# A fused attention and FFN kernel: seven block products for one FFN1, and a new order for batches 2 to 7

## The chip, the cores and the metric

One Trainium2 chip, one of its cores. The core has TensorE for matrix products (PE in the profile; its weight loads are PEld), VectorE (DVE), ScalarE (ACT), GpSimd (POOL, which here issues loads) and SyncE (SP, which here issues stores and transposing DMAs). SBUF is the working memory, PSUM the memory that TensorE writes: 8 banks of 512 float32 per partition. The metric is the device time of the kernel in microseconds; the median of several runs is given, and the profile shows one execution of its own.

## The reference

Attention with squared relu in place of softmax, then a two-layer FFN with a leaky relu. Cut to what matters:

```python
# q, k, v: 8 batches, 12 heads, 448 positions, head size 64
scores = scale * np.matmul(q, k.transpose(0, 1, 3, 2))
attn = np.maximum(scores, 0.0) ** 2 / S
x = np.matmul(attn, v)        # put together to 3584 tokens x 768
h = x @ w_in                  # 768 x 2048   (FFN1)
g = np.maximum(h, 0.0) + alpha * np.minimum(h, 0.0)
out = g @ w_out               # 2048 x 768   (FFN2), float32
```

## The kernel before

All products are in bfloat16 with sums in float32. The work of the eight batches is cut into pieces, and plans written as text say in which order the pieces are issued; each word of a plan issues one piece to the queues of its engines. Every engine takes its queue in order and waits where an operand or a buffer isn't ready.

**Attention.** Four heads of one batch are a quad of heads; there are 24. `load_qk` and `load_v` fetch them over POOL's queue. Before scores can be formed, q and k must lie transposed in a tile `T`. For the first five that is done on TensorE (`turn_pe`), from then on by `turn_dma` (L188): two copies, on ACT or DVE, rearrange q and k into a tile `perm` (L195; there is one such tile, three times the space of `w_mix` is used in its place), and a transposing DMA on SP's queue reads it (L197). `land` (L417) is a tiny POOL copy that waits for the landing; the loads of later quads are issued behind it on POOL. A quad has seven chunks of keys. A chunk's scores are four 64x64 products of 448 columns at once, over two PSUM banks (`score_mm`, L209); then comes the relu from PSUM, `rl`, on ACT (L218) or DVE (L220), and the square, `at`, on ACT (L229) or DVE (L231). When the seven squares are there, `attnv` multiplies them with v (28 products, L241) and two scalings write `xT` (L253 ACT, L255 DVE).

**FFN1.** Of a batch, 16 tiles of 128 hidden units: six products of 128x128 weights by 448 tokens each, into one bank (`f1_mm`, L275). Then ACT writes `neg` (L281) and DVE forms `gT` from it and from the bank (L282). 96 products per batch.

**FFN2.** Two batches share a `gT` of 896 columns, seven blocks of 128 tokens. Most blocks are taken in pairs (class `Pair`): the 2 x 2 blocks of a pair are multiplied with w_out by seven products of eight steps (384 columns each) and not eight, after Strassen and Winograd. The sums of blocks that this needs are made by DVE (`mix`, L331, and once for the weights in `weight_mix`, L313), and further DVE additions put the products together (`plus`, L340). A block that is in no pair goes through `f2` (L300). The stores go over SP's queue, 64 rows each, and near the end over ACT's too (the word `z`).

**PSUM.** The banks are given out as the plan is walked: `take_pair` and `take_bank` give the ones taken longest ago, `hold` keeps one for an accumulation.

**The order.** The first plans cover batches 0 and 1 and the first FFN2 blocks. Then come `FIRST_PAIR` for batch 2, `EACH` for batches 3, 4 and 6, `ONE_PAIR` for 5 and `LAST` for 7. In them `f` is an FFN1 tile, `cAAD` three chunks with relus on ACT, ACT and DVE, `s0D` a square, `v` an attention with its scalings, `p6` a product of the pair p with its addition, `pa` a sum, `n` or `nD` a quad's copies, transposing DMA, landing and next loads. `LAST` is batch 7's FFN1, 16 tiles, and behind it the two last pairs, 14 products. The last product is split into 256 and 128 columns (`p4e`).

Of the kernel before, what the change touches and what calls it, by code (L numbers as in the profile page):

```python
# [20 lines left out]
def kernel(  # L21
# [50 lines left out]
    paired, two_queues = [], []  # L72
# [17 lines left out]
    def hold_pair():  # L90
        lo = min((0, 2, 4, 6), key=lambda i: (max(taken[i], taken[i + 1]), i))
        taken[lo] = taken[lo + 1] = 10**9
        return lo

    def one():
        order = sorted(range(8), key=lambda i: (taken[i], i))
        free = [i for i in order if taken[i] < 10**9]
        if not paired:
            return order[0]
        mate = max(free, key=lambda i: taken[i]) ^ 1  # L100
        return mate if mate in order[:4] and taken[mate] < 10**9 else order[0]
# [86 lines left out]
    def turn_dma(n, eng="A"):  # L188
        if n in (5, 7, 8):
            w = w_mix[2 + n % 2].rearrange("p k c -> p (k c)")[:, :4 * NJ * D]  # L190
            p = w.rearrange("p (a j s d) -> p a j s d", a=2, j=NJ, s=2)
        else:
            p = perm_pool.tile([128, 2, NJ, 2, D], BF16, tag="perm", name="perm")
        for i, name in enumerate("qk"):
            (nc.vector.tensor_copy if eng == "D" else nc.scalar.copy)(p[:, i], raw.pop((n, name)).rearrange("p s j d -> p j s d"))  # L195
        t = T_pool.tile([128, 2, NJ, 128], BF16, tag="T", name="T")
        nc.sync.dma_start_transpose(out=t.rearrange("p a j c -> p (a j) c"),  # L197
                                    in_=p.rearrange("p a j s d -> p (a j s d)"))
        T[n] = t


    att, xT = {}, {}

    def score_mm(n, j):
        ps = take_pair()
# [28 lines left out]
    def attnv(n, eng="AD"):  # L234
        ps = take_pair()
        vv = vraw.pop(n)
        for j in range(NJ):
            a = att.pop((n, j))
            for r in range(2):
                for s in range(2):  # L240
# [3 lines left out]
                                     start=(j == 0), stop=(j == NJ - 1))  # L244
        b, g = divmod(n, NG)
        if g == 0:
            xT[b] = xT_pool.tile([128, NG, 2, S], BF16, tag="xT", name="xT")
        if eng == "A":
            nc.scalar.activation(xT[b][:, g], ps[:, :, :S], ACTF.Copy, scale=out_scale)
            return  # L250
        for r in range(2):
            if eng[r] == "A":
                nc.scalar.activation(xT[b][:, g, r], ps[:, r, :S], ACTF.Copy, scale=out_scale)  # L253
            else:
                nc.vector.tensor_scalar(xT[b][:, g, r], ps[:, r, :S], out_scale, None, ALU.mult)  # L255
# [15 lines left out]
    gT = singles.tile([128, KF, 2 * S], BF16, name="gT")  # L271

    def f1_mm(ps, b, ff, ks):
        for km in ks:
            nc.tensor.matmul(ps, w_in_sb[:, km // 2, km % 2, bass.ts(ff, 128)],  # L275
                             xT[b][:, km // 2, km % 2, :],
                             start=(km == 0), stop=(km == KM - 1))

    def f1_out(ps, b, ff):
        neg = neg_pool.tile([128, S], F32, tag="neg", name="neg")  # L280
        nc.scalar.activation(neg, ps, ACTF.Relu, scale=-1.0)  # L281
# [11 lines left out]
    def f2(sb, c, h, parts=None):  # L293

        first_col, width = COLS[h][0], COLS[h][1] - COLS[h][0]
        o = o_pool.tile([128, d_model - CUT], F32, tag="o", name="osb")
        for lo, hi in parts or ((0, width),):
            ps = take_bank()[:, :hi - lo]
            for ff in range(KF):
                nc.tensor.matmul(ps, gT[:, ff, bass.ts(c, 128)], w_out_sb[:, ff, first_col + lo:first_col + hi],  # L300
                                 start=(ff == 0), stop=(ff == KF - 1))
            nc.scalar.copy(o[:, lo:hi], ps)
            store(sb, c, first_col + lo, first_col + hi, o[:, lo:hi])


    def weight_mix(i, lo, hi):

        b11, b12 = w_out_sb[:, lo:hi, :NH], w_out_sb[:, lo:hi, NH:]
# [6 lines left out]
    class Pair:  # L315

        def __init__(self, a, b):
            self.a, self.b = a, b
            ga, gb = gT[:, :, bass.ts(a[1], 128)], gT[:, :, bass.ts(b[1], 128)]
            self.a11, self.a12, self.a21, self.a22 = ga[:, :KH], ga[:, KH:], gb[:, :KH], gb[:, KH:]  # L320
            self.s = {}

        def mix(self, *which):
            for i in which:
                t = self.s[2] if i == 4 else S_pool.tile([128, KH, 128], BF16, tag="S", name="S")
# [7 lines left out]
        def mm(self, ps, left, right, start):  # L333
            for i in range(KH):
                nc.tensor.matmul(ps, left[:, i], right[:, i], start=(start and i == 0), stop=(i == KH - 1),  # L335
                                 skip_group_check=not start)

        def plus(self, ps, u, keep=None):
            t = keep if keep is not None else o_pool.tile([128, d_model - CUT], F32, tag="o", name="osb")[:, :u.shape[-1]]
            nc.vector.tensor_tensor(t, ps, u, ALU.add)  # L340
            return t

        def kept(self, tag="u"):
            return u_pool.tile([128, NH], F32, tag=tag, name=tag)

        def p1(self):
            self.xb = hold()
            self.x = psum[:, self.xb, :NH]
            self.mm(self.x, self.a11, w_out_sb[:, :KH, :NH], True)
            self.m1 = self.kept("m")  # L350
            nc.scalar.copy(self.m1, self.x)

        def p2(self):
            self.mm(self.x, self.a12, w_out_sb[:, KH:, :NH], False)
            t = o_pool.tile([128, d_model - CUT], F32, tag="o", name="osb")[:, :NH]
            nc.scalar.copy(t, self.x)  # L356
            take(self.xb, 1)
            store(*self.a, 0, NH, t)

        def p6(self):  # L360
            y = take_bank()[:, :NH]
            self.mm(y, self.s[2], w_mix[1], True)
            self.u2 = self.plus(y, self.m1, self.kept())

        def p7(self):
            y = take_bank()[:, :NH]
            self.mm(y, self.s[3], w_mix[2], True)
            self.u3 = self.plus(y, self.u2, self.kept())

        def p5(self):  # L370
            self.zb = hold()
            self.z = psum[:, self.zb, :NH]
            self.mm(self.z, self.s[1], w_mix[0], True)
            store(*self.b, NH, d_model, self.plus(self.z, self.u3))

        def p4(self, parts=((0, NH),)):
            for lo, hi in parts:
                y = take_bank()[:, :hi - lo]
                self.mm(y, self.a22, w_mix[3][:, :, lo:hi], True)
                t = self.plus(y, self.u3[:, lo:hi])  # L380
                store(*self.b, lo, hi, t)

        def p4x(self, lo=0, hi=256):
            if lo == 0:
                self.o4 = o_pool.tile([128, d_model - CUT], F32, tag="o", name="osb")[:, :NH]
            y = take_bank()[:, :hi - lo]
            self.mm(y, self.a22, w_mix[3][:, :, lo:hi], True)
            self.plus(y, self.u3[:, lo:hi], self.o4[:, lo:hi])
            if hi == NH:
                store(*self.b, 0, NH, self.o4)  # L390

        def p4y(self):
            self.p4x(256, NH)

        def p4e(self):
            self.p4(((0, 256), (256, NH)))

        def p3(self):
            self.mm(self.z, self.s[4], w_out_sb[:, KH:, NH:], False)
            store(*self.a, NH, d_model, self.plus(self.z, self.u2))  # L400
            take(self.zb, 1)
# [6 lines left out]
    def prepare(n, eng="A"):  # L408
        if n < NQ:
            turn_dma(n, eng)  # L410
            land(n)
        if n + 2 < NQ:
            load_qk(n + 2)
        if n + 1 < NQ:
            load_v(n + 1)

    def land(n):  # L417
        nc.gpsimd.tensor_copy(landed, T[n][:1, 0, 0, :1])  # L418

    class Walk:  # L420

        def __init__(self):
            self.b, self.ff, self.held, self.parts, self.p, self.r, self.quad = 0, 0, [], 0, None, None, 11
# [9 lines left out]
        def step(self, w):  # L433
# [36 lines left out]
            elif c in "pr":  # L470
                if rest[0] in "abcd":
                    getattr(self, c).mix("abcd".index(rest[0]) + 1)
                else:
                    getattr(getattr(self, c), "p" + rest)()
# [3 lines left out]
            elif c == "g":  # L478
                f2(self.b // 2, int(rest[0]), int(rest[1]))
            elif c == "n":  # L480
                prepare(self.quad, rest or "A")
                self.quad += 1
# [21 lines left out]

    walk = Walk()
    walk("""Li0 Lv2 x02D x46A x24D x67A i6 t0q46D t0q24A t0q67A t0q02D t0k01D t0k24D t0k12A cA cD Lq3 cA Li1 t0k47D cA s1D t1q07D cAA s0D Li2 Lq4 s0D t1k07D cA s2D s1D Li3 y8 cAA s0D s0D cA cDA t2q07D s1D t2k05D cA s0D Lo0,0,8 s2D Lq5 Lv3 t2k57A Lo0,8 s0D Lv4 s0D cA cA cA Lv5 s0D s0D v cA v cA s0A cD e4 e1 s0D cD s0D cA s1A s1A e5 e4 e1 s0D e1 s0D v b t3q07A t3k07D E E E E""")
# [45 lines left out]
```

## Time and profile before

| | |
|---|---|
| median of 3 runs | 373.6 us (373.58 to 375.46) |
| profiled execution: span | 371.3 us |
| granted TensorE clock | 1.000 |
| PE busy | 363.6 us (98%) |
| DVE busy | 278.0 us (75%) |
| ACT busy | 274.7 us (74%) |
| POOL busy | 71.7 us (19%) |

An execution's own time holds some microseconds around the span. Busy PE is not PE at its peak: products are pipelined, and each counts as busy until its modelled end, so the pace is read from the starts. The chain of waits is followed back from the last instruction, at each step to what released it; its rows give start, length and what ran. In windows each engine's busy time in a stretch is given, with the number of instructions in brackets.

### The profile page before, as it was taken

Reading aid. Unit: us, or ns where it says so; the run is one execution under the profiler, and the core shown is the slowest. Engines: PE = TensorE matmul, PEld = TensorE weight load, DVE = VectorE, ACT = ScalarE, POOL = GpSimd, SP = SyncE. Lnnn points to the kernel's source line nnn. Section 1 sums busy time; section 2 is a strip of 40 time slices with the busy share of each in tenths; the row PEclk is TensorE's granted clock in tenths of the full one; section 3 lists DMA queues with packets and bytes.
Section 4 is the critical chain, followed back from the end, with each engine's and each line's share of the span. In section 5 each row is a group of like instructions: output and inputs, shape, how many; then the busy total and the mean of one; then the engine's idle time right before and its main releaser. Section 6 shows DMA issues by size and latency. Waiting matters only on the chain.

```text
span 371.3 us, 7894 instructions
## 1 busy us (share of the span) xinstructions
PE 363.6 (98%) x3105; PEld 197.5 (53%) x3105; DVE 278.0 (75%) x445; ACT 274.7 (74%) x406; POOL 71.7 (19%) x120
## 2 busy tenths in 40 slices
PE   8799999999999999999999999999999999999995
PEld 6454564444554565545555455554555455555563
DVE  3989988885968989566887768888749667856653
ACT  5998676877997678885997859967699866964400
POOL 8566150304211222022020220202200000000000
PEclk9999999999999999999999999999999999999999
DMA  9999989999999868455882659727646201220024
GB/s 143 188 203 202 199 135 191 153 160 167 180 171 150 123 96 163 92 89 90 160 144 64 99 80 168 144 56 121 111 89 134 49 2 43 65 65 0 0 64 108
DMA packets 73557, 43.29 MB, mean 117 GB/s; under 512 B 40368, under 2 KB 73008, under 8 KB 73520
## 3 DMA queue, kind: packets, MB, share of 16 engines
q0 software_dynamic: 27136, 22.58, 42.0%
q1 hardware_dynamic: 45712, 19.61, 25.9%
q10 hardware_dynamic: 672, 0.59, 0.5%
q8 instruction: 24, 0.39, 0.4%
q14 instruction: 13, 0.11, 0.1%
HBM read 45.62 MB, written 11.01 MB: 153 GB/s over the span
## 4 chain that ended last, share of the span: by engine, by line
PE 94%; DVE 2%; ACT 2%; issue 1%; ACTq 0%
PE psum L275 38%; PE psum L335 30%; PE psum L241 9%; PE psum L209 9%; PE psum L300 6%; PE psum L183 1%; PE psum L165 1%; DVE gT L282 1%; ACT rl L218 1%; ACT xT L253 1%; ACT neg L281 1%; DVE w_mix L195 1%; DVE T L186 0%; DVE at L231 0%; DVE osb L340 0%
## 5 line engine op out<-in xcount | busy, mean ns | idle before, releaser
L275 PE MATMUL psum<-xT,w_in_sb 128*128 128x448 bf16 x768 | 150.4, 353 | 0.2 <-DVE gT L282 0.2
L282 DVE SCALAR_TENSOR_TENSOR gT<-neg,beta_sb,psum 128x448 bf16<-128x448 f32 x128 | 85.3, 679 | 43.4 <-ACT neg L281 42.1
L218 ACT ACTIVATE rl<-psum 128x896 bf16<-128x896 f32 x128 | 111.2, 925 | 6.7 <-PE psum L209 4.7
L275 PEld LDWEIGHTS <-w_in_sb 128*128 128x128 bf16 x768 | 73.4, 98 | 73.0 <-issue 6.8
L281 ACT ACTIVATE neg<-psum 128x448 f32<-128x448 f32 x128 | 68.5, 547 | 41.0 <-PE psum L275 32.7
L231 DVE TENSOR_TENSOR at<-rl 128x896 bf16<-128x896 bf16 x105 | 62.2, 620 | 0.5 <-ACT rl L218 0.2
L229 ACT ACTIVATE at<-rl 128x896 bf16<-128x896 bf16 x63 | 58.6, 952 | 0.3
L335 PEld LDWEIGHTS <-S 128*128 128x128 bf16 x384 | 36.7, 98 | 28.4 <-issue 5.3
L335 PE MATMUL psum<-w_mix,S 128*128 128x384 bf16 x288 | 49.8, 326 | 0.2
L220 DVE TENSOR_SCALAR rl<-psum 128x896 bf16<-128x896 f32 x40 | 43.2, 1086 | 8.7 <-PE psum L209 8.1
L209 PE MATMUL psum<-T 64*64 64x448 bf16 x672 | 45.9, 357 | 2.0 <-DVE T L186 1.0
L418 POOL COPY landed<-T 1x1 bf16<-1x1 bf16 x18 | 3.3, 181 | 206.1 <-DMA T<-perm 182.9
L335 PEld LDWEIGHTS <-gT 128*128 128x128 bf16 x296 | 28.3, 98 | 20.2 <-issue 1.8
L241 PE MATMUL psum<-at,vraw 64*64 64x448 bf16 x672 | 36.6, 350 | 0.0
L335 PE MATMUL psum<-w_out_sb,gT 128*128 128x384 bf16 x192 | 34.0, 326 | 0.0
L340 DVE TENSOR_TENSOR osb<-psum,u 128x384 f32<-128x384 f32 (+2 forms) x37 | 20.2, 547 | 12.6 <-PE psum L335 8.2
L209 PEld LDWEIGHTS <-T 64*64 64x64 bf16 x672 | 17.4, 105 | 22.7 <-issue 14.8
L241 PEld LDWEIGHTS <-vraw 64*64 64x64 bf16 x672 | 21.2, 106 | 11.9 <-issue 2.9
L300 PE MATMUL psum<-w_out_sb,gT 128*128 128x256 bf16 (+1 forms) x128 | 22.0, 326 | 0.1
L255 DVE TENSOR_SCALAR xT<-psum 128x448 bf16<-128x448 f32 x24 | 14.9, 622 | 8.9 <-PE psum L241 8.3
L253 ACT ACTIVATE xT<-psum 128x448 bf16<-128x448 f32 x24 | 13.3, 556 | 9.1 <-PE psum L241 8.7
L356 ACT COPY osb<-psum 128x384 f32<-128x384 f32 x12 | 5.8, 480 | 17.4 <-PE psum L335 17.4
(45 smaller groups left out, 242.0 us busy)
## 6 DMA issues: line engine op xcount, KB each, us to landing
out_dram<-osb SPq DMA_DIRECT2D x91, 96.0 KB, 2.2
vraw<-in_v_dram POOLq DMA_DIRECT2D x24, 224.0 KB, 6.5
qraw<-in_q_dram POOLq DMA_DIRECT2D x23, 224.0 KB, 4.1
kraw<-in_k_dram POOLq DMA_DIRECT2D x23, 224.0 KB, 5.3
w_in_sb<-in_moe_w_in_dram POOLq DMA_DIRECT2D x16, 192.0 KB, 8.0
w_out_sb<-in_moe_w_out_dram POOLq DMA_DIRECT2D x4, 512.0 KB, 9.5
w_out_sb<-in_moe_w_out_dram POOLq DMA_DIRECT2D x4, 256.0 KB, 8.8
out_dram<-osb SPq DMA_DIRECT2D x8, 128.0 KB, 3.2
```

The lines of the kernel that those rows point to most:

```text
L209: nc.tensor.matmul(ps[64 * c:64 * c + 64, r, :S], t[64 * r:64 * r + 64, 1, j, 64 * c:64 * c + 64], t[64 * r:64 * r + 64, 0, :, 64 * c:64 * ...
L218: nc.scalar.activation(rl, ps[:, :, :S], ACTF.Relu)
L220: nc.vector.tensor_scalar(rl, ps[:, :, :S], 0.0, None, ALU.max)
L229: nc.scalar.activation(a, rl, ACTF.Square)
L231: nc.vector.tensor_tensor(a, rl, rl, ALU.mult)
L241: nc.tensor.matmul(ps[64 * s:64 * s + 64, r, :S], vv[64 * r:64 * r + 64, s, j, :], a[64 * r:64 * r + 64, s], start=(j == 0), stop=(j == NJ ...
L275: nc.tensor.matmul(ps, w_in_sb[:, km // 2, km % 2, bass.ts(ff, 128)], xT[b][:, km // 2, km % 2, :], start=(km == 0), stop=(km == KM - 1))
L281: nc.scalar.activation(neg, ps, ACTF.Relu, scale=-1.0)
L282: nc.vector.scalar_tensor_tensor(gT[:, ff, (b % 2) * S:(b % 2) * S + S], neg, beta_sb[:, ff:ff + 1], ps, ALU.mult, ALU.add)
L300: nc.tensor.matmul(ps, gT[:, ff, bass.ts(c, 128)], w_out_sb[:, ff, first_col + lo:first_col + hi], start=(ff == 0), stop=(ff == KF - 1))
L335: nc.tensor.matmul(ps, left[:, i], right[:, i], start=(start and i == 0), stop=(i == KH - 1), skip_group_check=not start)
L340: nc.vector.tensor_tensor(t, ps, u, ALU.add)
```

## The change

The plans for batches 0 and 1 and for the stage behind them issue the same pieces in the same order. Two things are new behind it.

First, batches 2 to 7 are one plan of some 960 words, read by a new class `Line`, in which each operation has a word of its own, with its PSUM bank: `f3` the six products of an FFN1 tile into bank 3, `N3` its `neg`, `G3` its `gT`; `c4` a chunk's scores into banks 4 and 5, `r4A` the relu on ACT, `s0D` a square; `v6` an attention, `x60A` and `x61D` its two scalings; `kqD` and `kkD` the copies of q and k, `t` the transposing DMA, the landing and the next loads; `+b63` product 6 of pair b into bank 3, `-b6` its addition or copy, `*ba` a sum. So a relu, a copy or an addition can be put anywhere among the products, and onto either engine.

Second, FFN1 of batch 7 is no longer 16 tiles of six products of 448 columns. Two tiles make a `Quad` (eight in all). Its weights are cut into 2 x 2 blocks (two tiles, two halves of the six steps) and the tokens into 2 x 2 blocks (two halves of the steps, two halves of the 448 tokens). A quad is then seven products of three steps and 224 columns. `w_in_mix` makes the sums of weight blocks (15 DVE operations; four for each of the eight quads, several at once), `tok_mix` the four sums of token blocks; they are kept in buffers whose earlier use is over. In a quad, `s`, `u` and `w` copy 224 columns of PSUM (capital letters: on DVE), `v` and `z` add on DVE, `n` is one relu of 896 columns on ACT, `g` and `h` are the two `gT`. The last two pairs of FFN2 follow as before, and the products of the two pairs before them stand among the quads'. The last product isn't split.

```diff
+    def w_in_mix(i, p, count, home):
+        a11, a12, a21, a22 = w_in_quarters(p, count)
...
+        x, y, op = {1: (a21, a22, ALU.add), 2: (made(1), a11, ALU.subtract),
+                    3: (a11, a21, ALU.subtract), 4: (a12, made(2), ALU.subtract)}[i]
+        nc.vector.tensor_tensor(t, x, y, op)
...
+    def tok_mix(i):
...
+        b11, b12, b21, b22 = x[:, :KI, :HS], x[:, :KI, HS:], x[:, KI:, :HS], x[:, KI:, HS:]
...
+        x, y, op = {1: (b12, b11, ALU.subtract), 2: (b22, tok_sum.get(1), ALU.subtract),
+                    3: (b22, b12, ALU.subtract), 4: (b21, tok_sum.get(2), ALU.subtract)}[i]
+        nc.vector.tensor_tensor(t, x, y, op)
...
+    class Quad:
...
+        def mm(self, ps, left, right, start):
+            for k in range(KI):
+                nc.tensor.matmul(ps, left[:, k], right[:, k], start=(start and k == 0), stop=(k == KI - 1),
+                                 skip_group_check=not start)
...
+            if c == "1":
+                self.mm(x[:, :HS], a11, b11, True)
+            elif c == "2":
+                self.mm(x[:, :HS], a12, b21, False)
+            elif c == "3":
+                self.mm(x[:, HS:S], self.w(4), b22, False)
+            elif c == "4":
+                self.mm(y[:, :HS], a22, tok_sum[4], False)
+            elif c == "5":
+                self.mm(x[:, HS:S], self.w(1), tok_sum[1], False)
+            elif c == "6":
+                self.mm(y[:, :HS], self.w(2), tok_sum[2], False)
+            elif c == "7":
+                self.mm(y[:, :HS], self.w(3), tok_sum[3], False)
+            elif c in "sS":
+                (nc.scalar.copy if c == "s" else nc.vector.tensor_copy)(y[:, :HS], x[:, :HS])
+            elif c in "uU":
+                (nc.scalar.copy if c == "u" else nc.vector.tensor_copy)(u[:, :HS], y[:, :HS])
+            elif c in "wW":
+                (nc.scalar.copy if c == "w" else nc.vector.tensor_copy)(u[:, HS:], y[:, :HS])
+            elif c == "v":
+                nc.vector.tensor_tensor(y[:, HS:S], x[:, HS:S], u[:, HS:], ALU.add)
+            elif c == "z":
+                nc.vector.tensor_tensor(x[:, HS:S], x[:, HS:S], u[:, :HS], ALU.add)
+            elif c == "n":
...
+                nc.scalar.activation(self.neg, psum[:, self.lo:self.lo + 2, :S], ACTF.Relu, scale=-1.0)
+            elif c in "gh":
...
+                nc.vector.scalar_tensor_tensor(gT[:, ff, (NB % 2) * S:(NB % 2) * S + S], self.neg[:, i],
+                                               beta_sb[:, ff:ff + 1], psum[:, self.lo + i, :S], ALU.mult, ALU.add)
...
+    class Line:
...
+        def do_k(self, w):
+            if self.perm is None:
+                self.perm = perm_pool.tile([128, 2, NJ, 2, D], BF16, tag="perm", name="perm")
+            copy = nc.vector.tensor_copy if w[1] == "D" else nc.scalar.copy
+            copy(self.perm[:, "qk".index(w[0])], raw.pop((self.quad, w[0])).rearrange("p s j d -> p j s d"))
+
+        def do_t(self, w):
+            n = self.quad
...
+            turn_rows(n, self.perm)
+            self.perm = None
+            land(n)
+            if n + 2 < NQ:
+                load_qk(n + 2)
+            if n + 1 < NQ:
+                load_v(n + 1)
+            self.quad += 1
...
+    P[4] = """s3D s4D s0A f0 c2 c4 s0A *ba r2A s1D c6 s0A r6D f1 f2 kqD N0 f3 kkD N2 G2 r4A f6 f7 N1 G0 N3 *bb G3 f0 N6 f2 +b63 G1 *bc G6 N0 N7 s2A c4 G0 t s0D G7
+c0 -b6 v6 r0D r4A N2 c4 G2 s1D c0 f3 r4A x60A *bd kqD f2 c4 r0A x61A r4A c0 N2 kkD f6 f7 r0D s3A G2 s1D f2 N6 c4 G6 s1A N7 s1D N2 c0 G7 f6 t r4A s1D
...
+r4A W222k W422k W144p r6A s1A f4 x21A N4 s1A f5 +h46 +h31 s2A s0D N5 s0D G4 f7 f4 v2 N0 G5 W242v -h4 f5 N7 -h3 x20D f6 x21D G0 f1 W442v N4 Q012 f0 G7
+N6 T1 G6 f7 f6 N1 W262v Q0S T2 Q06 G4 N0 f4 G1 N7 G0 N5 Q110 G7 G5 f7 f5 N6 Q1s Q02 *ic G6 N4 G4 N7 *jc N5 f6 G7 G5 f7 N7 N6 Q16 T3 +i14 T4 W462v G6
+W302 Q0u +i75 G7 Q1U -i1A +i24 -i2A *ia *ib W322 Q17 Q216 Q07 +i64 Q0W -i6 -i7 Q12 Q2s Q05 Q15 Q26 Q0v *ja *id +i54 Q2u Q03 Q0z +i45 Q04 Q1w Q1v Q0n
...
++k17 +l76 Q6g Q6h Q5n Q5g Q7n +k72 -k1A Q7g +l13 Q5h Q7h *ka +j44 *kb -j4 *la +k65 *lb -l1A -k6 +k50 -k7 +l61 *kd +k42 -k5 +k30 -k4 -l6 +l52 +k27 -k3
+-l7 -l5 +l46 *ld -k2D +l32 -l4 +l23 z -l3 -l2A"""
```

More of the change, by code (lines that the diff above doesn't have):

```diff
@@ L97, in one @@
         free = [i for i in order if taken[i] < 10**9]
[L98 to L101, printed above, removed]
+        return free[0]
     def take_bank():
@@ L271, with batches_of, may_write, may_read @@
     gT = singles.tile([128, KF, 2 * S], BF16, name="gT")
+    f1_done = {}
+    f2_done, f2_half = set(), set()
+    readers = {b: 0 for b in range(B)}
+    def batches_of(sb, c):
+        return {2 * sb + (128 * c) // S, 2 * sb + (128 * c + 127) // S}
+    for tile_no in range(B // 2 * NJ):
+        for b in batches_of(*divmod(tile_no, NJ)):
+            readers[b] += 1
+    def may_write(b, ff):
+        assert b < 2 or readers[b - 2] == 0, "gT is still read"
+        f1_done[(b, ff)] = True
+    def may_read(t, halves=(0, 1)):
+        for b in batches_of(*t):
+            for h in halves:
+                assert all((b, ff) in f1_done for ff in range(KF // 2 * h, KF // 2 * h + KF // 2)), "gT is not written"
+    def has_read(*tiles):
+        for t in tiles:
+            for b in batches_of(*t):
+                readers[b] -= 1
     def f1_mm(ps, b, ff, ks):
         for km in ks:
+            assert x_done[b] >= km // 2 + 1
+            f1_mm_done[b] = f1_mm_done.get(b, 0) + 1
             nc.tensor.matmul(ps, w_in_sb[:, km // 2, km % 2, bass.ts(ff, 128)],
@@ L291, in store, with f2_mm, f2_out, f2 @@
             eng.dma_start(out=rows[j][:, lo:hi], in_=t[64 * u:64 * u + 64])
[L293 to L303 removed]
+    def f2_mm(sb, c, h, i):
+        may_read((sb, c))
+        if (sb, c) in f2_half:
+            f2_done.add((sb, c))
+            has_read((sb, c))
+        f2_half.add((sb, c))
+        lo, hi = COLS[h]
+        for ff in range(KF):
+            nc.tensor.matmul(psum[:, i, :hi - lo], gT[:, ff, bass.ts(c, 128)], w_out_sb[:, ff, lo:hi],
+                             start=(ff == 0), stop=(ff == KF - 1))
+    def f2_out(sb, c, h, i):
+        lo, hi = COLS[h]
+        o = o_pool.tile([128, d_model - CUT], F32, tag="o", name="osb")
+        nc.scalar.copy(o[:, :hi - lo], psum[:, i, :hi - lo])
+        store(sb, c, lo, hi, o[:, :hi - lo])
+    def f2(sb, c, h):
+        i = one()
+        take(i, 1)
+        f2_mm(sb, c, h, i)
+        f2_out(sb, c, h, i)
+    mixed = [0] * 4
     def weight_mix(i, lo, hi):
+        assert not i or mixed[{1: 0, 2: 0, 3: 1}[i]] > mixed[i]
+        mixed[i] += 1
         b11, b12 = w_out_sb[:, lo:hi, :NH], w_out_sb[:, lo:hi, NH:]
@@ L331, in mix @@
                 nc.vector.tensor_tensor(t, x, y, op)
[L333 to L401, printed above, removed]
+        def run(self, name):
+            if name in "23":
+                i = self.held.pop({"2": "1", "3": "5"}[name])
+                take(i, 1)
+            elif name in "15":
+                i = self.held[name] = hold()
+            else:
+                i = one()
+                take(i, 1)
+            self.product(name, psum[:, i, :NH])
+            self.output(name)
```

272 lines of the change are left out of this document (223 added, 49 removed).

## The prediction

> **What bounds the kernel now.** I read the page's busy shares first, then the windows for the part that the change touches, then the chain of waits in that part. The change starts where batch 2 starts; in this execution that is 109.2 us after the span's start (the chain, further down, has the first products of its FFN1 there).
>
> ```profile
> PE 363.6 (98%) x3105; PEld 197.5 (53%) x3105; DVE 278.0 (75%) x445; ACT 274.7 (74%) x406; POOL 71.7 (19%) x120
> 109.20:371.30 262.10, 258.14 (x2036) 139.84 (x2032) 189.15 (x300) 187.71 (x278) 29.74 (x52) 1.00 0.51 93
> 109.20:152.50 43.30, 43.24 (x365) 23.33 (x361) 36.34 (x59) 33.24 (x49) 10.04 (x17) 1.00 0.85 139
> ```
>
> In a window the columns are the stretch, its length, then busy time of PE, weight loads, DVE, ACT and POOL, the granted clock, the DMA share and GB/s. PE is busy in 258.1 of the 262.1 us, and the 4 us that are missing lie at the end, behind its last product. The clock is 1.00. DVE has 72% and ACT 72%. In the first of these stretches DVE ran at 84% of the time (36.34 of 43.30) and PE lost nothing by it. So from batch 2 on TensorE sets the time: only fewer or shorter products, or shorter pauses between them, can shorten it, and only a pause that the new order puts in can lengthen it.
>
> A busy PE hides short pauses, because a product counts as busy until its modelled end. The chain shows them better (start, length, what). Here is one undisturbed run of attention work and one disturbed, and a second disturbed one:
>
> ```profile
> 109.25 9.19 PE psum L275 x48
> ...
> 143.82 0.53 ACT xT L253
> ...
> 176.83 0.31 PE psum L209 x4
> 177.14 1.32 PE psum L241 x28
> 178.47 0.38 PE psum L209 x8
> ...
> 186.25 0.69 PE psum L209 x12
> 186.94 1.52 PE psum L241 x28
> 188.47 0.53 ACT xT L253
> ...
> 189.04 0.97 PE psum L335 x5
> ...
> 283.61 0.69 PE psum L209 x12
> 284.30 1.50 PE psum L241 x28
> 285.80 0.70 PE psum L209 x12
> ...
> 322.40 0.53 ACT xT L253
> ...
> 331.09 18.27 PE psum L275 x96
> ```
>
> The 64x64 products of L209 and L241 go by fours, a four in 1.32 / 7 = 0.189 us. The run at 176.83 has ten fours and takes 178.47 + 0.38 - 176.83 = 2.02 us. The run at 186.25 (in the plan: three chunks, one attention, three chunks) has thirteen and takes 189.04 - 186.25 = 2.79, where 2.02 + 3 x 0.189 = 2.59 would do: a pause of 0.20, in which the chain goes over to ACT's writing of xT. The chain passes through that line four times from batch 2 on, the first at 143.82 and the last at 322.40. The run at 283.61, thirteen fours too, takes 285.80 + 0.70 - 283.61 = 2.89, a pause of 0.30. Together I count 4 x 0.20 + 0.30 = 1.1, with smaller ones **about 1.2 us of pauses**. That is all that a better order can win on PE here.
>
> **The change part by part.**
>
> *FFN1 of batch 7.* Its 96 products of 448 columns go; eight quads of seven products of three steps come, 168 of 224 columns. From the chain: 96x + e = 18.27 and 48x + e = 9.19 give x = 0.189 us a product and e = 0.11 us on coming from attention work. 224 columns don't occur; the nearest rows are these (the timeline and the groups by line):
>
> ```profile
> 10.44 0.62 PE L499 MATMUL psum<-idle 128*128 128x128 bf16 x8
> L499 PE MATMUL psum<-idle 128*128 128x128 bf16 x8 | 0.6, 220 | 0.0
> 353.09 4.06 PE L335 MATMUL psum<-w_mix,S 128*128 128x384 bf16 x24
> L335 PE MATMUL psum<-w_mix,S 128*128 128x384 bf16 x288 | 49.8, 326 | 0.2
> 366.09 1.48 PE L335 MATMUL psum<-w_mix,gT 128*128 128x256 bf16 x16
> L335 PEld LDWEIGHTS <-S 128*128 128x128 bf16 x384 | 36.7, 98 | 28.4 <-issue 5.3
> ```
>
> 128 columns: (0.62 - 0.220) / 7 = 0.057 us from start to start; 384: (4.06 - 0.326) / 23 = 0.162. The line between them gives 0.097 at 224, the line from 384 to 448 drawn on gives 0.095; I take 0.096. 168 x 0.096 = 16.1 against 96 x 0.189 = 18.2: **-2.1 us** (bounds -1.9 and -2.2). A weight load reads 98 ns, as long as such a product; but the row at 366.09 (eight products of 256 columns and eight of 128, each with weights of its own) needs (1.48 - 0.22) / 15 = 0.084, which is the line's value for their mean of 192, so the loads lie beside the products.
>
> [...]
>
> *The order of batches 2 to 7.* Each change between 64x64 and full products costs: behind a run e = 0.11, and in the run 0.69 - 3 x 0.189 = 0.12, together 0.23 us. Between the words that give PE full products, the old text has 28 runs of chunk and attention words, the new one 32. The counts of chunks (99), attentions (15), Strassen products of FFN2 (75) and FFN2 blocks (one, in two parts) are the same. So **+0.9 us**.
>
> *What DVE and ACT get.* Counted in the words: DVE takes 39 of 99 first relus, not 25, and 19 of 26 rearranging copies, not 8; five more output copies; squares stay. For batch 7 it gets 16 additions and 8 copies of 224 columns, 15 sums of w_in blocks (14 of 768 elements, one of 1536), 4 of tokens (672).
>
> ```profile
> L220 DVE TENSOR_SCALAR rl<-psum 128x896 bf16<-128x896 f32 x26 | 28.1, 1086 | 2.7 <-PE psum L209 2.3 <-issue 0.4
> L195 DVE COPY perm<-qraw 128x896 bf16<-128x896 bf16 x4 | 2.5, 612 | 0.0
> L340 DVE TENSOR_TENSOR osb<-psum,u 128x384 f32<-128x384 f32 x32 | 17.8, 557 | 10.9 <-PE psum L335 7.0 <-DMA out_dram<-osb 2.8
> L340 DVE TENSOR_TENSOR osb<-psum,u 128x256 f32<-128x256 f32 x1 | 0.4, 425 | 0.3 <-PE psum L335 0.3
> L331 DVE TENSOR_TENSOR S<-gT 128x1024 bf16<-128x1024 bf16 x22 | 14.5, 685 | 0.0
> ```
>
> 14 x 1.09 + 11 x 0.61 + 5 x 0.56 = 24.7. The 224-column ones, by the slope between 256 and 384, take 0.39: 24 x 0.39 = 9.4. The sums, scaled from 685 ns at 1024 elements, about 0.5 each, the long one 1.0: 19 of them 10. Added: some 44 us of durations; the busy time grows by less, since queued DVE operations overlap a little (I take 5 off): from 189 to about 228 of 261 us, 87%. ACT loses 14 relus and 11 copies. On the path this costs nothing as long as PE has products that don't wait for it: FFN1 tiles of batch 6 and the 14 products of pairs i and j (8 x 0.162 = 1.30 us each) stand between the quads' steps. If that cover is gone, each pause is like the 0.2 to 0.3 above. 87% is little over the 84% that the first stretch bore with no loss, so I take the same 1.2 us of pauses as before: **0** (bounds -1.2 and +5, the rivals below).
>
> *Rearranging copies, transposes, loads.* There is one perm tile, so a copy waits until the last transpose has landed. A copy that waits holds all that is queued behind it on DVE: relus, squares and gT, and so the banks that PE needs next.
>
> ```profile
> L197 SPq DMA_TRANSPOSE T<-perm x16: 1296/1532/3163, 62.3 to 292.5; - x16
> DMA to landing us min/median/max: 3.9/4.1/12.0
> ```
>
> From a transpose's issue to its landing 4.1 us pass (median). In the new text the words between a quad's second copy and the next quad's first hold at least 6.2 us of PE's work at the durations above, and at least 10 us lie before the quad's first chunk. SP issues a transpose in order among the stores, and POOL issues the next loads behind the landing, as before; none of them is late by these numbers. 0.
>
> *The end.* The old end is a product in two halves with two additions; the new one adds product 2 onto product 1 and copies 384 columns on ACT.
>
> ```profile
> 363.49 1.46 PE L335 MATMUL psum<-w_out_sb,gT 128*128 128x384 bf16 x8
> 365.03 0.48 ACT L356 COPY osb<-psum 128x384 f32<-128x384 f32 x1 [11.26 <-PE psum L335]
> 367.16 0.74 DVE L340 TENSOR_TENSOR osb<-psum,u 128x256 f32<-128x256 f32 x2 [0.26 <-PE psum L335]
> out_dram<-osb SPq DMA_DIRECT2D x91, 96.0 KB, 2.2
> out_dram<-osb ACTq DMA_DIRECT2D x3, 96.0 KB, 2.4
> out_dram<-osb SPq DMA_DIRECT2D x1, 32.0 KB, 1.9
> ```
>
> Old: PE ends at 366.09 + 1.48 = 367.57, DVE at 367.90, 0.33 later. Such a copy ended 365.51 - 364.95 = 0.56 after PE: +0.2. The last stores grow from 32 to 96 KB: +0.3 to +0.5. **+0.6 us.**
>
> Sum: -2.1 + 0.9 + 0 + 0.6 = -0.6. The profiled execution has a span of 371.3, the median of the runs is 373.6, so 2.3 lie around it. **371.3 - 0.6 + 2.3 = 373.0 us.**
>
> **The rivals.**
>
> *The pauses go.* The new order spaces chunks and their relus over four bank pairs and spares ACT, which the chain passed at the pauses. Against it: more work on DVE. 373.0 - 1.2 = 371.8, and 371.3 if the end costs only 0.2.
>
> *DVE becomes the pace-maker; slower.* Place: the attention runs, 15 with an attention. A bank pair waits for a relu of 1.09 on DVE in place of 0.92 on ACT, behind whatever the queue holds, and the attention needs its seven squares. For it: in the stretch from 61 to 71 us DVE is full and PE stands in the chain behind DVE and ACT.
>
> ```profile
> 61.00:71.00 10.00, 9.88 (x61) 4.78 (x59) 9.65 (x17) 6.90 (x13) 3.10 (x5) 1.00 1.02 154
> 68.08 1.27 DVE gT L282 x2
> 69.35 1.05 DVE w_mix L195 x2
> L218 ACT ACTIVATE rl<-psum 128x896 bf16<-128x896 f32 x75 | 65.5, 917 | 5.8 <-PE psum L209 3.8 <-ACT rl L218 2.0
> ```
>
> DVE has 9.65 of these 10 us (PE's 9.88 is by modelled ends), and from 68.08 to 70.40 the chain lies on DVE alone. Price: each of the 15 at the larger pause, 15 x 0.30 = 4.5, in place of 1.2: +3.3, 376.3. It turns the change into a loss as soon as all pauses come to more than 1.8 us.
>
> *The quads run dry; slower too.* A quad's products hang on four copies or additions between them, some 0.45 each with their hop (0.56 at 384 columns). Eight quads have 32 of them, 14 us; if a quarter finds no other product to run, +3.6: 376.6.
>
> *Weight loads set the pace of the narrow products.* One after the other at the row's 98 ns, 168 loads take 16.5 us in place of 16.1: 373.4; if each waited for the end of the product before it, 16.5 us more: 389. The 57 ns at 128 columns speak against both. [...]
>
> *The copies wait for a landing after all*: a transpose of 12.0 us, the row's maximum, against the 6.2 in hand, would hold DVE nearly 6 us once; PE's cover of perhaps half gives 376.
>
> **How the numbers follow.** Forecast (372.2 to 374.3) 0.44; the pauses go 0.29; DVE paces 0.18; quads dry 0.06; paced by loads 0.01; late landing 0.02. The range leaves out the last two and some of the outer ends: 371.3 to 376.4. 0.5% (1.9 us) is about what a measurement of this kernel can tell from no change. Faster by over that (below 371.7) is under two thirds of the second case, 0.19; slower by over that (above 375.5) most of the third to sixth and little else, 0.23; the rest 0.58.
>
> **What would show it.** Right: starts of the 224-column products 0.096 us apart; 32 runs with 0.23 of extra each; PE's last product about 1.2 us earlier and the last store landing about 0.6 us later behind it; the chain still on PE all through batches 2 to 7. Wrong: DVE lines in the chain between 109 and 330 us, PE waiting on rl or at; PE waiting on ACT or DVE copies among the quads; POOL or DVE waiting on T<-perm with PE behind them. A fall below 371 us would mean that the old order lost more between products than the chain shows.

## The result and the profile after

The new kernel takes 371.65 us (median of 7 runs, 371.28 to 372.47); the old one, in runs of the same session, 373.54. The ratio is 0.995, with a 95% interval of 0.9933 to 0.9968: faster by 1.9 us. The forecast was 373.0, in a range of 371.3 to 376.4. The result lies where the rival "the pauses go" had put it, at 371.8.

The page of the new kernel, its busy times with their shares of the span:

```profile
PE 361.2 (98%) x3169; PEld 201.7 (55%) x3169; DVE 310.9 (84%) x513; ACT 256.3 (69%) x388; POOL 73.0 (20%) x120
```

and the view of windows, the stretch from batch 2 on (same columns as before):

```profile
109.20:369.50 260.30, 255.89 (x2096) 144.04 (x2095) 222.26 (x368) 169.22 (x260) 30.53 (x52) 1.00 0.52 94
```

The span is 369.5 us, 1.8 less. From batch 2 on DVE has 222.3 of 260.3 us, 85% (72% before), ACT 65%. PE is as dense as before. So the same reading holds: what counts is the number and length of the products and the pauses between them. The chain shows both; first two attention runs, then batch 7's last quads:

```profile
188.60 0.50 PE psum L206 x8
189.10 1.32 PE psum L237 x28
190.42 0.38 PE psum L206 x8
190.80 1.24 PE psum L303 x6
...
286.33 0.69 PE psum L206 x12
287.03 1.32 PE psum L237 x28
288.35 0.38 PE psum L206 x8
288.73 1.24 PE psum L303 x6
...
342.71 3.16 PE psum L501 x33
345.87 11.71 PE psum L379 x72
```

L206, L237, L303, L379 and L501 are the new lines of chunks, attentions, FFN1 tiles, FFN2 products and quads. The run at 188.60 has eleven fours and takes 190.80 - 188.60 = 2.20 us, which is 11 x 0.189 + 0.12: no pause. The run at 286.33, the longest of the new order (three chunks, an attention, two), has twelve and takes 2.40 = 12 x 0.189 + 0.13: none either. By the starts of PE's products all 32 runs are like that. Two pauses are left, both at the opening of the stretch: 0.29 us ahead of batch 2's first FFN1 tile, which waits for `xT` (the old kernel did not pause there), and 0.23 us near 112 us. The first stands in PE's timeline, with its idle time in brackets:

```profile
109.42 1.29 PE L303 MATMUL psum<-xT,w_in_sb 128*128 128x448 bf16 x6 [0.25 <-ACT xT L249]
```

Read by the starts too, 21 of the old kernel's 28 runs are undisturbed (0.13 us over their fours), and seven pause, by 0.13 to 0.31 us, 1.57 us in all. By the chain the prediction had counted 1.2. A quad's products start 3.16 / 33 = 0.096 us apart.

So the four terms measure as follows, from the two profiled executions:

| term | forecast | measured |
|---|---|---|
| batch 7's FFN1 | -2.1 | 168 x 0.096 - 96 x 0.189 = -2.0 |
| 32 runs in place of 28 | +0.9 | 4 x 0.23 = +0.9 |
| pauses | 0 | 0.52 in place of 1.57, by the starts: -1.05 |
| the end | +0.6 | +0.4 |
| sum | -0.6 | -1.75 (spans: -1.8, medians: -1.9) |

The end, from the timeline of the new kernel:

```profile
363.91 1.46 PE L379 MATMUL psum<-w_out_sb,gT 128*128 128x384 bf16 x8
365.45 0.48 ACT L392 COPY osb<-psum 128x384 f32<-128x384 f32 x1 [13.86 <-DMA out_dram<-osb]
```

PE ends at 365.37 and the copy at 365.93, 0.56 later, as forecast (0.33 before). The bracket names the landing of an earlier store, at 365.43, as what came last before the copy; in the run of the same kernel at the end of this study it was PE, with the copy as close behind it, so the landing cost nothing here. The span ends 369.5 - 365.93 = 3.6 us behind the copy; in the old kernel it ended 371.3 - 367.90 = 3.4 behind the last addition. The larger stores cost 0.1 to 0.2, not 0.3 to 0.5.

### The profile page after: what moved, and what is told of

Same layout as the page of the kernel before. It is cut to its first block, busy times and chain, and to the rows that moved or that the text cites. A ratio compares the mean times of both kernels' runs of the same rounds, so it can differ in the third digit from the quotient of the medians.

```text
span 369.5 us, 8035 instructions
## 1 busy us (share of the span) xinstructions
PE 361.2 (98%) x3169; PEld 201.7 (55%) x3169; DVE 310.9 (84%) x513; ACT 256.3 (69%) x388; POOL 73.0 (20%) x120
## 4 chain that ended last, share of the span: by engine, by line
PE 89%; DVE 3%; ACT 3%; DMA 2%; issue 2%; SPq 1%; ACTq 0%; POOLq 0%
PE psum L303 32%; PE psum L379 28%; PE psum L206 9%; PE psum L237 9%; PE psum L330 6%; PE psum L501 4%; ACT rl L215 1%; DMA kraw<-in_k_dram 1%; DMA out_dram<-osb 1%; DVE gT L311 1%; ACT neg L310 1%; DVE w_mix L188 1%; PE psum L175 1%; SPq L320 1%; DVE T L178 0%
## 5 line engine op out<-in xcount | busy, mean ns | idle before, releaser
L303 PE MATMUL psum<-xT,w_in_sb 128*128 128x448 bf16 x672 | 134.5, 353 | 0.5 <-ACT xT L249 0.3
L215 ACT ACTIVATE rl<-psum 128x896 bf16<-128x896 f32 x114 | 100.9, 929 | 20.0 <-PE psum L206 15.9
L303 PEld LDWEIGHTS <-w_in_sb 128*128 128x128 bf16 x672 | 63.4, 98 | 65.2 <-issue 10.0
L217 DVE TENSOR_SCALAR rl<-psum 128x896 bf16<-128x896 f32 x54 | 58.5, 1086 | 11.3 <-PE psum L206 10.5
L653 ACT ACTIVATE neg<-psum 128x448 f32<-128x448 f32 x80 | 43.1, 547 | 23.7 <-PE psum L303 12.5
L659 DVE SCALAR_TENSOR_TENSOR gT<-neg,beta_sb,psum 128x448 bf16<-128x448 f32 x80 | 53.0, 676 | 7.6 <-ACT neg L653 6.4
L379 PEld LDWEIGHTS <-S 128*128 128x128 bf16 x384 | 36.7, 98 | 26.4 <-issue 3.4
L379 PE MATMUL psum<-w_mix,S 128*128 128x384 bf16 x288 | 51.0, 326 | 0.0
L206 PE MATMUL psum<-T 64*64 64x448 bf16 x672 | 46.5, 357 | 1.7 <-ACT rl L215 0.9
L435 POOL COPY landed<-T 1x1 bf16<-1x1 bf16 x18 | 4.8, 267 | 182.4 <-DMA T<-perm 158.8
L379 PEld LDWEIGHTS <-gT 128*128 128x128 bf16 x288 | 27.6, 98 | 20.0 <-issue 2.5
L237 PE MATMUL psum<-at,vraw 64*64 64x448 bf16 x672 | 36.2, 350 | 0.0
L379 PE MATMUL psum<-w_out_sb,gT 128*128 128x384 bf16 x192 | 34.9, 326 | 0.0
L396 DVE TENSOR_TENSOR osb<-psum,u 128x384 f32<-128x384 f32 x36 | 19.7, 553 | 12.0 <-PE psum L379 7.1
L206 PEld LDWEIGHTS <-T 64*64 64x64 bf16 x672 | 16.8, 105 | 23.1 <-issue 15.8
L237 PEld LDWEIGHTS <-vraw 64*64 64x64 bf16 x672 | 20.1, 107 | 12.5 <-issue 1.7
L311 DVE SCALAR_TENSOR_TENSOR gT<-neg,beta_sb,psum 128x448 bf16<-128x448 f32 x32 | 21.0, 677 | 3.9 <-ACT neg L310 3.3
L310 ACT ACTIVATE neg<-psum 128x448 f32<-128x448 f32 x32 | 17.2, 548 | 8.8 <-PE psum L303 6.1
L330 PE MATMUL psum<-w_out_sb,gT 128*128 128x512 bf16 (+1 forms) x128 | 22.0, 326 | 0.1
L249 ACT ACTIVATE xT<-psum 128x448 bf16<-128x448 f32 x28 | 15.5, 557 | 4.5 <-PE psum L237 4.5
```

What stands on the lines that cost most here:

```text
L206: nc.tensor.matmul(ps[64 * c:64 * c + 64, r, :S], t[64 * r:64 * r + 64, 1, j, 64 * c:64 * c + 64], t[64 * r:64 * r + 64, 0, :, 64 * c:64 * ...
L215: nc.scalar.activation(rl, ps[:, :, :S], ACTF.Relu)
L217: nc.vector.tensor_scalar(rl, ps[:, :, :S], 0.0, None, ALU.max)
L237: nc.tensor.matmul(ps[64 * s:64 * s + 64, r, :S], vv[64 * r:64 * r + 64, s, j, :], a[64 * r:64 * r + 64, s], start=(j == 0), stop=(j == NJ ...
L311: nc.vector.scalar_tensor_tensor(gT[:, ff, (b % 2) * S:(b % 2) * S + S], neg, beta_sb[:, ff:ff + 1], ps, ALU.mult, ALU.add)
L330: nc.tensor.matmul(psum[:, i, :hi - lo], gT[:, ff, bass.ts(c, 128)], w_out_sb[:, ff, lo:hi], start=(ff == 0), stop=(ff == KF - 1))
```

## The experiments

Two questions were open. What is each part worth by itself? And why did the pauses go, though DVE took 33 us more: because of where the operations stand, because ACT was relieved, or because 85% is still far from DVE's edge? Ratios below are to the old kernel, run beside each; the new kernel once more, at the end, gave 0.9953 (0.9934 to 0.9972).

### The order without the seven products

```diff
-            if c == "1":
-                self.mm(x[:, :HS], a11, b11, True)
+            if c in "16":
+                for km in range(KM):
+                    nc.tensor.matmul((x if c == "1" else y)[:, :S],
+                                     w_in_sb[:, km // 2, km % 2, bass.ts(2 * p + (c == "6"), 128)],
+                                     xT[NB][:, km // 2, km % 2, :], start=(km == 0), stop=(km == KM - 1))
```

and in the plan all words `W` and `T` go, and of the `Q` words all but 1, 6, n, g and h.

> The new order with batch 7's FFN1 as 16 tiles of six 448-column products, put where the quads' products 1 and 6 stood; the sums of w_in and of tokens and the quads' copies and additions are left out, all else as in the new kernel. Theory (PE sets the time, the seven products are worth their columns): PE's last product 96 x 0.189 - 168 x 0.096 = 2.05 us later, 371.65 + 2.05 = 373.7, still without pauses in the attention runs. Rival (the quads' chains and DVE work cost something that the trace hides): less than that is lost, about 1 us, 372.7.

Measured: 373.68 us, ratio 1.0002 (0.9977 to 1.0028), as the theory had it. The seven products are worth 2.0 us, what their columns say; the quads' copies, additions and sums cost nothing. And the new order without them takes as long as the old one: it buys 1.0 us of pauses with four more runs (0.9) and a longer end (0.4).

### The price of a run

The old kernel, with two runs of three chunks cut in each of batches 3, 4 and 6 (the cuts in `EACH`):

```diff
-f f f f s2A f s1D cAAA s1D f f
+f f f f s2A cA f s1D cAA s1D f f
-p6 s0D pd p7 n cA rc s1A cAA
+p6 s0D pd cA p7 n rc s1A cAA
```

> The old kernel, in whose plan for batches 3, 4 and 6 two runs of three chunks are cut into one and two chunks with a product or a tile between them: six runs more, the same operations. Theory (each change between 64x64 and full products costs 0.23 us by itself): PE's last product 6 x 0.23 = 1.4 us later, 374.9. Rival (the extra on either side is only the profile's way of marking the starts): no change, 373.5 within 0.5.

Measured: 375.67 us, ratio 1.0071 (1.0049 to 1.0092), 2.6 us slower, more than the 1.4 of six runs and far from the rival's no change. The profile shows where the rest is:

```profile
162.34 0.70 ACT rl L218
163.04 0.55 ACT neg L281
163.61 0.69 DVE gT L282
164.30 0.04 issue
164.34 3.56 PE psum L275 x18
```

Behind the cut run PE waits for a bank: a relu, a `neg` and a `gT` are done one after another before it may go on. There are three such pauses, one in each of the three batches, by the starts 0.29 us each: 1.4 + 0.9 = 2.3. So the price of a run holds, and a shifted chunk also shifts the operations behind it on ACT and DVE.

### Shorter runs in the old order

```diff
-pd cA p7 rb n p5 s2D
+pd p7 cA rb n p5 s2D
-v cAD s1D s1A s3A cA s3A r6 s2A r7
+v cAD s1D s1A s3A r6 cA s3A s2A r7
```

> The old kernel, in whose plans for batches 2, 3, 4 and 6 the last chunk of a run of three chunks, an attention and three chunks is moved behind the next product, so that no bank pair is wanted twice within a run there: four runs more. Theory (a run with six chunks pauses because banks and squares are not ready, 0.15 to 0.3 us; a shorter one does not): the four pauses go, 1.0 us, and four changes of product kind come, 0.9 us: 373.5 within 0.4, with no pause above 0.1 us in those runs. Rival (the pauses come from ACT's load, wherever the chunks stand): the pauses stay and the runs come on top, 374.5.

Measured: 373.87 us, ratio 1.0017 (1.0005 to 1.003), 0.6 us slower. The run that paused at 186.25 in the old kernel now reads so in the chain:

```profile
186.64 0.69 PE psum L209 x12
187.33 1.48 PE psum L241 x28
188.81 0.38 PE psum L209 x8
189.18 1.41 PE psum L335 x8
190.59 0.31 PE psum L209 x4
```

Twelve fours in 189.18 - 186.64 = 2.54 us: 0.15 over 12 x 0.189 + 0.12. By the starts it was 0.28 in the old kernel (the chain had shown 0.20 of it), and the four pauses together fall from 0.96 to 0.52 us. They are halved, not gone, and the single chunk at 190.59 costs its change of product kind. Neither side is right: the length of a run matters, and it isn't all.

### The new order, the old division between ACT and DVE

Fourteen `r` words and eleven `k` words get an A for their D, for example:

```diff
-c0 -b6 v6 r0D r4A
+c0 -b6 v6 r0A r4A
```

> The new order word for word, but 14 first relus and 11 rearranging copies go from DVE back to ACT, as the old plans had them (25 relus and 8 copies on DVE). Theory A (the pauses went because of where chunks, relus and scalings stand): 371.65 within 0.5, no pauses in the attention runs. Theory B (they went because ACT was relieved): pauses of 0.2 to 0.3 us come back at half of the 15 attention runs or more, at least +1.5, 373.2 or more.

Measured: 383.31 us, ratio 1.0274 (1.0258 to 1.029): 11.7 us over the new kernel. The window of that stretch:

```profile
109.20:381.10 271.90, 259.33 (x2095) 145.31 (x2095) 202.97 (x343) 187.75 (x285) 30.36 (x52) 1.00 0.49 89
```

a piece of its chain of waits:

```profile
186.13 0.34 PE psum L206 x4
...
187.31 0.93 ACT perm L693
188.24 0.83 ACT rl L215
189.07 0.04 issue
189.11 0.38 PE psum L206 x4
```

and PE in its timeline at the same place (start, duration, what, products, and in brackets the idle time before with what ended it):

```profile
187.79 0.36 PE L206 MATMUL psum<-T 64*64 64x448 bf16 x4
189.11 0.38 PE L206 MATMUL psum<-T 64*64 64x448 bf16 x4 [0.96 <-ACT rl L215]
189.43 2.77 PE L379 MATMUL psum<-w_mix,S 128*128 128x384 bf16 x16
```

A rearranging copy now stands on ACT ahead of a relu whose bank PE needs. From 187.31 to 189.07 the chain lies on ACT, on the copy and then the relu, and the next four of scores begin 189.11 - 187.79 = 1.32 us behind the last, where 0.189 is the pace: a pause of 1.1 us. Reckoned so over the whole stretch, the pauses come to over 11 us. They came back, as theory B had it, and much larger. But DVE is busy 202.97 of 271.9 us, 75%, and ACT 187.75, 69%; the old order had 72% and 72% and paused for 1.57 us. So it isn't the load of an engine: an operation given to the other queue at the same word stands among other neighbours there.

### How much load DVE bears

First 12 relus more for DVE (every fifth `r` of ACT), then the same load spread evenly:

```diff
+                if count == 3:
+                    count = 0
+                    nc.vector.tensor_copy(idle, w_out_sb[:, 0, :128])
```

> The new kernel with 12 of the 60 first relus that ACT has given to DVE, every fifth one: DVE +12 x 1.0 us, from 85% to about 90% of its stretch. Theory (DVE has room until it is nearly full): no pause over 0.1 us, 371.65 within 0.5. Rival (87% was the edge, as the prediction's slower case had it): a pause of about 0.3 us at each of the 12, 375.2.

> The new kernel with a copy of 128x128 bfloat16 put into DVE's queue behind every third of its operations from batch 2 on, about 120 in all, some 10 to 15 us of DVE time spread evenly, no operation moved to another engine. DVE comes to about 90% of the stretch, as in the run with 12 relus more. Theory (a moved relu costs through its place in the other engine's queue, not through DVE's load): at most +3 us, below 374.7. Rival (DVE was at its edge at 85%): +10 us or more, 381 or more, as in that run.

Measured: the 12 relus, 387.43 us, ratio 1.0396 (1.0352 to 1.044); the padding, 371.43 us, ratio 0.995 (0.9934 to 0.9966), as fast as the new kernel. For the relus, neither the theory (within 0.5 us of 371.65) nor the rival (375.2) had anything like that. The window of the stretch, with the relus:

```profile
109.20:388.30 279.10, 261.66 (x2095) 145.89 (x2095) 233.85 (x380) 159.67 (x248) 31.58 (x52) 0.99 0.51 89
```

with the padding:

```profile
109.20:369.00 259.80, 256.13 (x2099) 144.81 (x2096) 232.60 (x488) 169.35 (x260) 30.68 (x52) 1.00 0.53 95
```

and the padding itself, in the view of groups by line (us in all and ns of one, idle time before):

```profile
L646 DVE COPY idle<-w_out_sb 128x128 bf16<-128x128 bf16 x120 | 23.4, 195 | 0.0
```

DVE is busy 232.6 us with the padding, 90% of the stretch, and 233.9 with the relus. The first costs nothing, the second 15.8 us. So a busy share of 90% does not by itself hold PE up.

That leaves the place in the queue. In the new kernel's trace an operation's place in the plan is not its time: at the twelve relus, the DVE operation that stands ahead in the plan ended between 2.7 us before and 3.2 us after the relu's start on ACT. Moved to DVE, a relu either waits there for work that ACT had been ahead of, or holds that work until its scores are there. So twelve were taken at which the two queues stand at the same time:

> The new kernel with 12 first relus moved from ACT to DVE, as many as in the run with 12 relus more, but those at which, by the new kernel's trace, the DVE operation ahead in the plan ends between 0.2 us before and 0.5 us after the relu's start on ACT; in that run the twelve stood between 2.7 us before and 3.2 us after. Theory (what costs is a relu's place among the operations of the other queue): under a third of that run's loss, at most 376. Rival (twelve relus of 1.09 us are too much for DVE wherever they stand): 383 or more.

Measured: 377.91 us, ratio 1.0117 (1.0089 to 1.0146). DVE is busy 234.1 us, the same again, and 6.3 us are lost in place of 15.8. That is two fifths, not the third that the theory wanted, but far from the rival's 383. What PE's scores wait for, by the view of waits from 109 us on (who, for whom, us in all, times, longest), in the run with every fifth relu:

```profile
PE psum L206 <- DVE rl L217: 4.4, 3, 2.7
PE psum L206 <- DMA T<-perm: 2.5, 1, 2.5
```

and with the twelve that fit:

```profile
PE psum L206 <- DVE rl L217: 2.8, 5, 0.6
```

The longest wait for a relu falls from 2.7 to 0.6 us. So with one load of DVE, 232.6 to 234.1 us, the time is 371.4, 377.9 or 387.4: what counts is which operations make up the load and where they stand. The two sets of relus differ in their places alone (two of the twelve are the same in both); the padding differs in kind as well, since nothing waits for it. (The profiled execution with every fifth relu took 390.1 us, and 2.5 of that is a landing that was late in it, below.) What the remaining 6.3 us come from, the relu's own 1.09 us at one place or further shifts behind it, stays open.

### The copies directly behind the transposes

```diff
-s0A c4 G0 t s0D G7
-c0 -b6 v6 r0D r4A N2 c4 G2 s1D c0 f3 r4A x60A *bd kqD f2
+s0A c4 G0 t kqD kkD s0D G7
+c0 -b6 v6 r0D r4A N2 c4 G2 s1D c0 f3 r4A x60A *bd f2
```

and so for all quads of heads from the thirteenth on.

> The new kernel with both rearranging copies of a quad directly behind the transposing DMA of the quad before, so that they wait for its landing with the engine's queue behind them. A transpose lands some 4.1 us after its issue. Theory (a waiting copy holds the relus, squares and gT behind it, and PE runs out of banks): 1 to 3 us of PE pauses at each of the twelve copies that stand early, in all 10 to 25 us, 382 to 397. Rival (8 banks cover the wait): within 1 us of 371.65.

Measured: 386.21, 387.22 and 391.42 us, and 392.55 us for the profiled execution; ratio 1.0405 (1.0329 to 1.0482), by the middle one of the three 15.6 us over the new kernel, as the theory had it. From the profiled execution's waits:

```profile
DVE perm L693 <- DMA T<-perm: 12.9, 6, 4.5
```

DVE stands six times before a copy, up to 4.5 us, which is about a transpose's 4.1 from issue to landing. ACT stands once, for 2.3 us. Waiting is not all of the loss in this execution: for 10.2 us of it the granted clock was at 0.50, and its mean over the 390.8 us of the span was 0.984. The distance between a landing and the next copies is worth some 16 us if it is missing. It is no gain over the old order, in which from 109 us on POOL's tiny copies alone waited for a transpose's landing.

### The end and the start

Product 4 last and in halves, as the old kernel ended:

```diff
-+l46 *ld -k2D +l32 -l4 +l23 z -l3 -l2A
++l23 *ld -k2D +l32 -l2A z -l3 E64
```

where `E64` is product 4 in 256 and 128 columns, into banks 6 and 4, with its additions and stores.

> The new kernel with another end: product 2 of the last pair goes ahead of product 3, and product 4 comes last in halves of 256 and 128 columns in two banks, each with its addition on DVE and its stores, as the old kernel ended. Theory (the new end costs 0.2 us by the copy and 0.2 to 0.3 us by the larger last stores): 0.3 to 0.6 us less, 371.2. Rival (the end is set by the queue of stores on SyncE): no change, 371.65.

Measured: 371.87 us, ratio 0.9977 (0.9952 to 1.0003): no gain. The timeline near the end:

```profile
364.51 1.48 PE L729 MATMUL psum<-w_mix,gT 128*128 128x256 bf16 x16
365.58 0.74 DVE L731 TENSOR_TENSOR osb<-psum,u 128x256 f32<-128x256 f32 x2 [0.32 <-PE psum L729]
367.55 0.56 SPq L320 DMA_DIRECT2D out_dram<-osb  x1
```

The last addition ends at 366.32, but its store is issued by SyncE at 367.55, 1.2 us later: the queue of stores, in which this one took 0.56 us to issue, is the limit now, as the rival had it. In that execution PE also waited 0.4 us for a landing. The next two change the queues, without and with the halves, the second also with `f1` ahead of the first chunks:

```diff
--l7 -l5 +l46 *ld -k2D +l32 -l4 +l23 z -l3 -l2A
+-l7 z -l5 +l46 *ld -k2D +l32 -l4 +l23 -l3 -l2A
```

> The new kernel with only the last edit of the three: ACT's queue takes half of the stores from product 5 of the last pair on, not from the last two outputs. Theory (with the product whole, the last copy on ACT ends 0.56 us behind PE and its stores go out at once, so SyncE's queue is no limit): no change, 371.65 within 0.3. Rival (the queue is the limit there too): 0.4 us less.

Measured: 371.49 us, ratio 0.9954 (0.9932 to 0.9975): no change, as expected.

```diff
-s3D s4D s0A f0 c2 c4 s0A *ba r2A s1D c6 s0A r6D f1 f2
+s3D s4D s0A f0 f1 c2 c4 s0A *ba r2A s1D c6 s0A r6D f2
--l7 -l5 +l46 *ld -k2D +l32 -l4 +l23 z -l3 -l2A
+-l7 z -l5 +l23 *ld -k2D +l32 -l2A -l3 E64
```

> The new kernel with three edits: the tile f1 goes ahead of the first chunks, so that they come 1.1 us later behind the landing of their transposes; the last product comes in halves as in the run with another end; and ACT's queue of stores is used from product 5 of the last pair on, seven outputs before the end. Theory (at the end SyncE's queue of stores was the limit once the product was split; at the start the first chunks stand just behind a landing): the last store's issue follows its addition within 0.1 us, 0.4 to 0.6 us less than the new kernel, 371.1, and no run with PE waiting on a landing. Rival (the end is set by the landings of the stores alone): no change, 371.65.

Measured: 371.7 us, ratio 0.9963 (0.9938 to 0.9987): no gain. Its last addition ends 0.35 us behind PE, at 366.38, and the span 3.4 behind that, so the end did become 0.3 to 0.4 us shorter than the new kernel's, though the last stores are issued 0.3 and 0.4 us behind the addition, not within 0.1. But the chain shows what took it back:

```profile
112.03 0.34 PE psum L206 x4
112.38 0.02 issue
112.40 0.93 ACT rl L215
113.33 0.04 issue
113.37 4.70 PE psum L303 x24
```

With `f1` moved, tile f2 follows the chunks directly and needs the bank of the first, whose relu has just begun: 0.6 us. The halves with two queues and without moving `f1` weren't tried; they should give some 0.4 us, too little for these intervals.

> The new kernel once more, to stand beside these on the same chip and to see whether the landing that the first chunks wait for is late in some executions. Theory: 371.65 within 0.4; a landing 0.4 to 2.5 us late in one execution of several.

Measured: 371.65 us, ratio 0.9953; the profiled execution had no wait for a landing. Of the executions profiled in this study with the new start unmoved, three of ten had one (2.5 us in the run with every fifth relu, 0.4 with product 4 in halves, 0.3 with the twelve that fit). Its cause is in two rows, POOL's tiny copy behind a landing and the first chunks on PE, in the new kernel

```profile
110.09 0.18 POOL L435 COPY landed<-T 1x1 bf16<-1x1 bf16 x1 [6.95 <-DMA T<-perm]
110.65 0.76 PE L206 MATMUL psum<-T 64*64 64x448 bf16 x12
```

and in the old one:

```profile
109.47 0.18 POOL L418 COPY landed<-T 1x1 bf16<-1x1 bf16 x1 [7.24 <-DMA T<-perm]
118.36 0.76 PE L209 MATMUL psum<-T 64*64 64x448 bf16 x12
```

The quad of heads that the new order opens with lands at about the same time as before, but is wanted 0.6 us behind its landing, no longer 8.9.

## Why the prediction was right, and where it was off

The direction and the range held, and TensorE does set the time from 113 us to its last product. At the opening, from 109.3 to 112.7, the chain lies on ACT; behind 357.6 it follows the stores, by the near tie at the last copy, while PE goes on without a pause. Point by point:

- **Batch 7's FFN1**, -2.1: measured -2.0, by the starts (0.096 us at 224 columns) and by taking it out. The line drawn through the rows at 128, 384 and 448 columns gave the pace. The weight loads did lie beside the products: the new kernel's profile shows one of 98 ns for each of the 168, and the products start 0.096 us apart all the same.
- **The order**, +0.9 for four runs: right. The old kernel with six runs more lost at least that per run.
- **"I take the same 1.2 us of pauses as before: 0"** is the step that failed: by the starts the pauses fell from 1.57 to 0.52 us. The sum came out 1.0 short by it, and what I had as the second case was what happened. The 1.2 was itself too small: three pauses counted at 0.20 us were 0.28 by the starts, and two, of 0.13 and 0.17 us, were not counted. Two of 0.13 us stand in the very stretch that I read as bearing 84% with no loss. The reason I gave for keeping the pauses, DVE at 87%, came out near (85%) and does not bear on it: 90% cost nothing.
- **The end**, +0.6: +0.4; the copy was right, the larger stores cost 0.2 to 0.3 less than taken.
- **DVE as pace-maker**: falls in the form given. Its price was not too high, though: twelve relus given to the other queue cost 6 to 16 us, by their places, where I had allowed 3.3.
- **The copies**: no wait for a landing in the plan's own quads, as said. I counted only quads whose copies stand in the new plan; the one before them, with 0.6 us in hand, I missed.

Why the pauses went is shown only in part. Shorter runs halve four of them in the old order; the new order's division between the engines is needed too, since the same words with the old division pause for some 11 us. Which single placement ends which pause was not taken apart, and that the new plan names each operation's bank, where the old one hands out those taken longest ago, was not tried by itself.

## What to carry to other kernels

Where TensorE is dense, price a change by its columns and by the changes between kinds of product, each from rows of the trace; both held here within 0.1 us. An engine's share of busy time says little about whether it will hold up TensorE: 120 small operations spread over its queue, for which nothing waited, cost nothing, 12 relus in wrong places 16 us and 12 in better places still 6. In a plan for queues taken in order, the place of an operation and its engine are one decision, and text order is not time order: look up when both queues get there before moving one.

## What the runs showed of the hardware that was not expected

Behind a pause of PE of 2.73 us the granted clock came down to 0.50 for 3.4 us. In the run with every fifth relu on DVE, PE in the timeline around its longest pause:

```profile
228.23 0.36 PE L206 MATMUL psum<-T 64*64 64x448 bf16 x4
231.31 0.38 PE L206 MATMUL psum<-T 64*64 64x448 bf16 x4 [2.73 <-DVE rl L217]
231.63 4.41 PE L379 MATMUL psum<-w_mix,S 128*128 128x384 bf16 x16
```

and windows there (the clock is the third number from the end):

```profile
228.20:231.10 2.90, 0.39 (x11) 0.11 (x1) 2.89 (x4) 0.00 (x0) 0.00 (x0) 1.00 0.08 11
231.10:232.00 0.90, 0.69 (x6) 0.32 (x6) 0.90 (x3) 0.70 (x1) 0.00 (x0) 0.77 0.00 0
232.00:235.50 3.50, 3.50 (x14) 1.73 (x13) 2.01 (x5) 3.50 (x6) 0.00 (x0) 0.57 0.00 0
235.50:240.00 4.50, 4.50 (x34) 2.41 (x32) 2.73 (x5) 4.34 (x6) 0.80 (x2) 1.00 0.79 160
```

PE was idle for 2.73 us. The granted clock, 1.00 in the first window, is 0.77 and 0.57 in the next two and 1.00 again from 235.5. The 16 products of 384 columns behind the pause took 4.41 us; the same group behind a pause of 0.96 us took 2.77, in the timeline of the old division shown above. So this pause cost 1.6 us more behind it.

The length of a pause alone did not decide there. In the same execution the clock came down a second time: in the window from 289.60 to 293.02 it is 0.50, as it is from 231.58 to 234.99, though the pause ahead of it was of 1.67 us only (from 286.64). Three other pauses, of 2.51 us from 110.99, 1.67 from 202.37 and 1.84 from 247.37, were followed by no fall. What sets off a fall was not shown. Two stretches of 3.4 us at a clock of 0.50 are some 3.4 us of work lost, an estimate from their length and clock; the mean clock of this execution, 0.991 over 388.3 us, gives 3.5. That is part of why the misplaced relus cost so much, and a reason to keep even rare pauses short.
